# Attention on two row halves of the TensorE array: weighted sums on one half, float32 scores in 32-row strips on the other

## The chip, the cores and the metric

The kernel runs on one core of one Trainium2 chip. A core has a matrix engine (TensorE, "PE" in the profile, with its weight loads as "PEld"), a vector engine (VectorE, "DVE"), an activation engine (ScalarE, "ACT"), a general engine (GpSimd, "POOL") and SyncE ("SP"), which issues most of the DMAs here. Matrix products read SBUF and write PSUM, which has eight banks of 128 x 512 float32. The metric is the device time of one execution in microseconds (us); smaller is better. All inputs and outputs are float32.

## The reference

A block with two branches on the same normalised input, 2048 tokens of width 448: attention with 16 query heads of width 28 that share one key and one value head, and an MLP of width 1792 behind a second normalisation.

```python
def _A_ref(x, wq, wk, wv, wo):
    B, S, D = x.shape                       # 1, 2048, 448
    H = 16
    Dh = D // H                             # 28
    q = (x @ wq).reshape(B, S, H, Dh).transpose(0, 2, 1, 3)
    k = x @ wk
    v = x @ wv
    scores = jnp.einsum("bhqd,bkd->bhqk", q, k) * (Dh ** -0.5)
    p = _softmax(scores, axis=-1)
    o = jnp.einsum("bhqk,bkd->bhqd", p, v)
    return o.transpose(0, 2, 1, 3).reshape(B, S, H * Dh) @ wo

def _B_ref(x, w1, b1, w2, b2):
    y = _layernorm(x, axis=-1)
    h = _gelu(jnp.einsum("bsd,df->bsf", y, w1) + b1)
    return jnp.einsum("bsf,fd->bsd", h, w2) + b2

xn = _layernorm(x, axis=-1)
return x + _A_ref(xn, wq, wk, wv, wo) + _B_ref(xn, w1, b1, w2, b2)
```

## The kernel before

The program is written in one function, `block_kernel`, with the order of the instructions of each engine set by hand (`manual_schedule`). Matrix products that need float32 accuracy are done in two ways. Some take float32 operands as they are; the profile shows two records for each such product. Others split an operand into a high and a low half of the type float32r and add three products of halves, one record each.

**Projection** (0 to 66 us). For each of four chunks of 512 tokens, `norm_parts` normalises and transposes the rows, and `q_slot` computes four groups of 128 columns of queries, keys and values. Its `evac` copies a group's high half to `qe[:, 0, :]` (L396), and `low` subtracts to get the low half `qe[:, 1, :]` (L403). Group 0 holds the value and the key. Four DMAs spread the key's halves over four blocks of 32 rows of `ks` (high, high, low, low in an order that pairs with the queries' blocks), and the halves of the queries go to two tensors in DRAM, `qd[0]` and `qd[1]`.

**MLP** (66 to 352 us). 56 slots, each `mlp1` (eleven products into a bank of the ring `ra`, then the gelu on ScalarE and VectorE) and, two slots later, `mlp2` (twelve products into four banks that stay open). In the last two slots `then` puts a score behind each group of three products, eight scores in all (`EARLY`).

**Attention** (352 to 893 us). The work is cut into 16 units of four heads and 512 queries, a unit into 16 key tiles of 128 keys. For each key tile and head, `scores` does one product over all 128 rows (L616): the three products of halves, 28 rows each, and a row that carries the shift of the exponent stand one above the other in the 128 rows. It lands in a bank of the rings `ra` and `rb` (three each, taken in turn), and ScalarE turns it into weights with an exponential (L618), which are float32 in SBUF. `pv` multiplies the weights of a key tile by the values, 32 columns with a column of ones for the sum (L731): four float32 products, one for each head, each over 128 rows and on its own 32 columns of the array, all adding into the one bank `po`.

The loop (L820) goes in steps of two key tiles: eight scores, and then `weighted()` with the eight weighted sums of the step before. Small jobs hang on slots between the scores: the load of the next unit's queries (`load_unit`, eight DMAs), its running maximum over the first 32 keys (`find_max`, one product, L537, then VectorE and a DMA that writes the shift row), the normalisation of the last unit (`norm_jobs`: a copy out of the bank, a DMA of the sums, a reciprocal, two DMAs through DRAM that spread it, a multiplication and the split into halves), and the output projection (`o_parts`, twelve products of 448 columns a unit into the bank `mo`, L694 to L698, one to three a step as `PARTS` says). `last_norm` finishes the last unit. Behind it stands a branch (`outside`) that recomputes all units with the true maximum if a sum left its limits; in the execution profiled here it is not taken.

The scores' order, the wait for a bank and the weighted sums are these lines:

```python
s = score_bank()
pe.matmul(s, ks[:, kt * P:(kt + 1) * P], qss[u][:, j, :], start=True, stop=True)
p = early.pop(0) if early else att.tile([P, CW], F32, name="p", bufs=WEIGHTS)
act.activation(p, s, AF.Exp, scale=SCALE)
```

Of the kernel before, what the change touches and what calls it, by code (L numbers as in the profile page):

```python
# [18 lines left out]
P = 128  # L19
# [13 lines left out]
WEIGHTS = 28  # L33
EARLY = 8
PARTS = 2, 1, 2, 1, 2, 2, 2
# [4 lines left out]
def block_kernel(ctx, tc, x, wq, wk, wv, wo, w1, b1, w2, b2, out):  # L40
# [8 lines left out]
    mo = ctx.enter_context(tc.tile_pool(name="mo", bufs=1, space=PSUM))  # L49
# [63 lines left out]
    def bank(shape):  # L113
        return mo.tile(shape, F32, name="mo")

# [17 lines left out]
    make_identity(nc, ident)  # L133
    one = keep.tile([P, 3], F32, name="one")
# [5 lines left out]
    pool.memset(f(ks), 1.0)  # L140
    pool.memset(f(kd), 0.0)
    pool.memset(f(qm), 0.0)
# [129 lines left out]
    def norm_parts(c, second, first=False, bank=mtile):  # L272
        again, second = second, second or c in KEPT
        xh = xt_p.tile([P, 4, CW], F32R, name="xh")
        xl = xl_p.tile([P, 4, CW], F32R, name="xl")
        xts[c, second and c not in KEPT] = xh, xl
        xns = {}

        def center(k):
            t = CT * c + k  # L280
            if first:
                xn = f(wqp.tile([P, 2, CW], F32R, name="qe", bufs=5))[:, 0, :]
            else:
                xn = (wqp if k % 2 and not again else tmp).tile([P, 4 * P], F32, name="xn", bufs=1)
            scale, bias = (lnq, lnqb) if second else (lnr, lnb)
            src = lines.pop(t) if again else xin[t]
            act.activation(xn[:, 0:D], src, AF.Identity, bias=bias[:, t:t + 1], scale=scale[:, t:t + 1])
            xns[k] = xn

            def doubled():  # L290
                (pool if 0 < c else dve).tensor_scalar(
                    xn[:, D:512], src[:, 384:448], scale[:, t:t + 1], bias[:, t:t + 1], op0=ALU.mult, op1=ALU.add)

            if first and k == 1:
                return doubled
            doubled()

        def turn(k, lows=None):
            sl = slice(k * P, (k + 1) * P)
            pt = bank([P, 4, P])  # L300
            for b in range(4):
                pe.transpose(pt[:, b, :], xns[k][:, b * P:(b + 1) * P], ident)  # L302
            act.activation(xh[:, :, sl], pt, AF.Copy)
# [80 lines left out]
    def q_slot(c, i):  # L384
# [7 lines left out]
        def evac():  # L392
            qe = wqp.tile([P, 2, CW], F32R, name="qe", bufs=5)
            if c in KEPT:
                dve.tensor_mul(ps, ps, ibs[c])
            act.activation(qe[:, 0, :], ps, AF.Copy)  # L396
            vt = None
            if i == 0:
                vt = wqp.tile([32, CW], F32, name="vt", bufs=1)
                act.activation(vt, ps[0:32, :], AF.Copy)  # L400

            def low():
                dve.tensor_sub(qe[:, 1, :], ps, f(qe[:, 0, :]))  # L403
                if i == 0:
                    for dst, j in ((32, 0), (0, 1), (64, 1), (96, 0)):
                        nc.sync.dma_start(f(ks[dst:dst + DH, cols]), f(qe[32:60, j, :]))
                    for h in range(4 if c == 0 else 0):
                        nc.sync.dma_start(f(kd[32 * h:32 * h + DH, 32 * h:32 * h + 32]), f(qe[32:60, 0, 0:32]))
# [105 lines left out]
    qss, ots, qst = {}, {}, []  # L514

    def clear_q():
        qst.append(xt_p.tile([P, 4, CW], F32R, name="xh"))
        pool.memset(f(qst[-1]), 0.0)

    def load_q(u, qs):  # L520
        c, g = units[u]
        for blk, i in ((1, 0), (2, 0), (0, 1), (3, 1)):
            src = qd[i][4 * DH * g:4 * DH * (g + 1), c * CW:(c + 1) * CW].rearrange("(j r) n -> r j n", r=DH)
            nc.sync.dma_start(f(qs[32 * blk:32 * blk + DH]), src)

    def load_strips(u):
        c, g = units[u]
        for j in range(4):
            rs = slice(DH * (4 * g + j), DH * (4 * g + j + 1))
            nc.sync.dma_start(f(qm[32 * j:32 * j + DH, :]), qd[0][rs, c * CW:(c + 1) * CW])  # L530
# [4 lines left out]
    def block_max(keys, dst):  # L535
        pm = bank([P, CW])
        pe.matmul(pm, keys, qm, start=True, stop=True)  # L537
# [3 lines left out]
    def shift_rows(u, mr):  # L541
        mn = keep.tile([P, CW // 32], F32R, name="mn", bufs=2)
        dve.tensor_scalar(mn, mr, -1.0, 0.0, op0=ALU.mult, op1=ALU.add)
        dve.transpose(blocks(tm), f(mn)[:, :, None].to_broadcast([P, CW // 32, 32]))
        nc.sync.dma_start(f(qss[u][60:61, :, :]), tm[DH:P:32, :])

    def load_unit(u):
        qss[u] = qst[u % 2]
        load_strips(u)
        load_q(u, qss[u])  # L550

    def find_max(u):
        mr = keep.tile([P, CW // 32], F32, name="mr", bufs=2)
        block_max(kd, mr)
        shift_rows(u, mr)

    ring_a = ctx.enter_context(tc.tile_pool(name="ra", bufs=3, space=PSUM))
# [30 lines left out]
    def mlp2(c, ft, then=None):  # L588
# [5 lines left out]
        for k in range(CT):  # L594
# [8 lines left out]
            if then is not None:  # L603
                then()
# [4 lines left out]
    todo = [(u, kt, j) for u in range(NU) for kt in range(NT) for j in range(4)]  # L609

    def score_bank():
        return ring_b[0].tile([P, CW], F32, name="t") if ring_b and next(turn_s) % 2 else spare()

    def scores(u, kt, j):
        s = score_bank()
        pe.matmul(s, ks[:, kt * P:(kt + 1) * P], qss[u][:, j, :], start=True, stop=True)  # L616
# [10 lines left out]
    for n in range(len(mslots) + 2):  # L627
# [12 lines left out]
        if (c, ft) == (NCH - 1, 1):  # L640
            clear_q()
            clear_q()
# [10 lines left out]
        if n >= len(mslots):  # L653
            t = f(xl_p.tile([P, 4, CW], F32R, name="xl"))
            early.extend(t[:, k, :] for k in range(4))
            mlp2(*mslots[n - 2], then=lambda: scores(*todo.pop(0)))
# [6 lines left out]
    ring_b.append(ctx.enter_context(tc.tile_pool(name="rb", bufs=3, space=PSUM)))  # L663
    op = ctx.enter_context(tc.tile_pool(name="op", bufs=1, space=PSUM))
# [40 lines left out]
    def norm_jobs(u, po):  # L705
        c, g = units[u]
        oc = att.tile([P, CW], F32, name="oc")
        dve.tensor_copy(oc, po)  # L708
# [18 lines left out]
    def pv(u, kt):  # L727
        if kt == 0:
            pos[u] = op.tile([P, CW], F32, name="po")
        for j in range(4):  # L730
            pe.matmul(pos[u][32 * j:32 * j + 32, :], vs[:, kt, :], ps[u, kt, j],  # L731
                      start=(kt == 0), stop=(kt == NT - 1))
# [31 lines left out]
    side = {}  # L764

    def at(step, job, slot=4):
        side.setdefault((min(step, PER * NU - 1), slot), []).append(job)
# [9 lines left out]
    at(3, split_out)  # L777
    waiting = []

    def weighted():  # L780
        for u, kt in waiting:
            pv(u, kt)
        if not waiting or waiting[-1][1] < NT - 1 or u == NU - 1:
            return
        norm = norm_jobs(u, pos.pop(u))
        next(norm)
        for d in (1, 3):
            at(PER * (u + 1) + d, lambda: next(norm), 3)
        parts = []

        def part():
            if not parts:
                parts.append(o_parts(*units[u]))
            next(parts[0])

        for d, n in enumerate(PARTS if u < NU - 2 else (3, 3, 3, 3)):
            for slot in (1, 5, 7)[:n]:
                at(PER * (u + 1) + 4 + d, part, slot)
# [10 lines left out]
    def flag(last):  # L809
# [5 lines left out]
        pf = bank([1, 1])  # L815
# [3 lines left out]
    done = EARLY  # L819
    for step in range(PER * NU):  # L820
        for i in range(8):
            if done:
                done -= 1
            else:
                scores(*todo.pop(0))
            for job in side.pop((step, i), []):
                job()
        weighted()
        waiting = [divmod(n, NT) for n in (2 * step, 2 * step + 1)]
    extremes(sums[:, 0:NU - 1, :].rearrange("p u e -> p (u e)").bitcast(I32), worst)  # L830
    weighted()
    tc.mark_branch_hint_location("outside", hint="LikelyTaken")
    last_norm(NU - 1, pos.pop(NU - 1), flag)

    outside = nc.values_load(count)
    with tc.If(outside > 0, preferred_fallthrough_block=True, label="outside"):
        ka = att.tile([P, 8, P], F32R, name="ka", bufs=1)
        mx = att.tile([P, CW // 32, S // 32], F32, name="mx", bufs=1)
        pool.memset(f(ka), 0.0)
        for u in range(NU):  # L840
            load_unit(u)
            for n in range(S // 32):
                for h in range(4 if n % 8 == 0 else 0):
                    nc.sync.dma_start(f(ka[32 * h:32 * h + DH, :, 32 * h:32 * h + 32]),
                                      f(blocks(ks[32:32 + DH, 32 * n:32 * n + 256])))
                block_max(ka[:, n % 8, :], mx[:, :, n])
# [3 lines left out]
            for kt in range(NT):  # L850
                for j in range(4):
                    scores(u, kt, j)
                pv(u, kt)
            for _ in norm_jobs(u, pos.pop(u)):
# [28 lines left out]
```

## Time and profile before

| | us |
|---|---|
| median of 3 runs (lowest, highest) | 906.45 (904.81, 907.35) |
| the profiled execution | 906.6 |
| its span, from the first to the last instruction | 904.8 |
| projection | 0 to 66 |
| MLP | 66 to 352.4 |
| attention | 352.4 to 892.6 |
| end | 892.6 to 904.8 |

The columns of the lines below are told where they are shown. A record of a group names its line, engine, operation, what it writes and reads, its form, and its count; busy time and the mean of one instruction in ns follow. In the time-ordered view the first number is the start in us and the second the length; a bracket tells how long the engine was idle before and what ended that. The form of a matrix product is rows * columns of the array that it uses: 128*128 is the whole array, 128*32 one group of 32 columns. The ends of matrix products are modelled, so distances between starts are used for what one costs.

### The profile page before, as it was taken

How to read it: one execution, taken by the hardware profiler on the slowest of the kernel's cores; microseconds unless marked ns; L12 is line 12 of the kernel's file. 1: busy time of each engine (PE TensorE's matmuls, PEld its weight loads, DVE VectorE, ACT ScalarE, POOL GpSimd, SP SyncE). 2: the span in 40 equal slices, each digit the busy share in tenths (PEclk: the TensorE clock that was granted, in tenths of full speed). 3: DMA queues.
4: the chain of work that ended last, by engine and by line, in shares of the span. 5: the costliest groups of instructions: out<-in, count | busy, mean ns of one | idle time of the engine just before them, and what ended most of it. 6: DMA issues, size and time to landing. Idle time of an engine off the chain costs nothing.

```text
span 904.8 us, 13015 instructions
## 1 busy us (share of the span) xinstructions
PE 889.1 (98%) x4925; PEld 567.7 (63%) x4925; DVE 293.7 (32%) x554; ACT 676.6 (75%) x1285; POOL 156.4 (17%) x149
## 2 busy tenths in 40 slices
PE   8989999999999999999999999999999999999996
PEld 8867888888888887454454454455455455455452
DVE  7865455335345342222122122122122122122123
ACT  5764443433443437999999999999999999999993
POOL 6443343233235331000000000000000000000000
PEclk9999999999999999999999999999999999999999
DMA  9791112002001303402202222202222112232001
GB/s 299 203 280 49 42 62 82 1 0 82 19 23 52 71 11 106 112 26 54 50 26 54 76 82 54 50 25 54 81 76 54 48 29 54 73 84 54 1 13 45
DMA packets 42047, 60.08 MB, mean 66 GB/s; under 512 B 10795, under 2 KB 26745, under 8 KB 41977
## 3 DMA queue, kind: packets, MB, share of 16 engines
q1 hardware_dynamic: 40568, 58.60, 22.8%
q8 instruction: 41, 0.67, 0.3%
q10 hardware_dynamic: 1408, 0.57, 0.2%
q14 instruction: 30, 0.24, 0.1%
HBM read 43.16 MB, written 14.80 MB: 64 GB/s over the span
## 4 chain that ended last, share of the span: by engine, by line
PE 94%; DVE 2%; ACT 1%; issue 0%; DMA 0%; POOL 0%; ACTq 0%; DVEq 0%; POOLq 0%
PE po L731 26%; PE s L616 16%; PE m L596 14%; PE t L616 13%; PE s L178 12%; PE qp L178 3%; PE mo L694 1%; PE mo L696 1%; PE mo L698 1%; PE s L181 1%; PE s L183 1%; PE qp L302 0%; DVE hz L579 0%; PE mo L537 0%; PE qp L181 0%
## 5 line engine op out<-in xcount | busy, mean ns | idle before, releaser
L618 ACT ACTIVATE p<-s 128x512 f32<-128x512 f32 x508 | 315.5, 621 | 26.7 <-PE s L616 22.3
L618 ACT ACTIVATE p<-t 128x512 f32<-128x512 f32 x508 | 319.5, 629 | 0.0
L731 PE MATMUL po<-p,vs 128*32 128x512 f32 x2032 | 244.1, 598 | 0.0
L616 PE MATMUL s<-xh,ks 128*128 128x512 f32 x516 | 216.6, 420 | 0.0
L616 PE MATMUL t<-xh,ks 128*128 128x512 f32 x508 | 200.4, 394 | 0.3 <-DVE a L601 0.3
L616 PEld LDWEIGHTS s<-xh,ks 128*128 128x128 f32 x516 | 97.0, 188 | 121.6 <-ACT p L618 105.6
L731 PEld LDWEIGHTS po<-p,vs 128*32 128x32 f32 x2032 | 53.1, 109 | 121.4 <-issue 116.1
L577 ACT ACTIVATE hx<-s,b1t 128x512 f32<-128x512 f32 x56 | 38.5, 688 | 115.3 <-PE s L183 105.6
L700 DVE TENSOR_TENSOR row<-row,mo 128x448 f32<-128x448 f32 x60 | 37.3, 621 | 235.9 <-PE mo L698 234.7
L585 POOL TENSOR_TENSOR hl<-hx,hh 128x512 fp32r<-128x512 f32 x56 | 77.6, 1386 | 184.1 <-DVE hh L584 175.0
L722 POOL TENSOR_TENSOR otl<-oc,oth 128x512 fp32r<-128x512 f32 x15 | 19.4, 1292 | 500.5 <-DVE oth L721 266.3
L616 PEld LDWEIGHTS t<-xh,ks 128*128 128x128 f32 x508 | 95.5, 188 | 14.0 <-ACT p L618 1.9
L596 PE MATMUL m<-w2l,hh 128*128 128x448 f32 x224 | 82.6, 369 | 0.9 <-DVE w2l L380 0.9
L596 PE MATMUL m<-w2h,hl 128*128 128x448 f32 x224 | 82.0, 366 | 0.7 <-POOL hl L585 0.7
L596 PE MATMUL m<-w2h,hh 128*128 128x448 f32 x224 | 82.3, 367 | 0.2 <-DVE a L601 0.2
L579 DVE SCALAR_TENSOR_TENSOR hz<-hz,hx 128x512 f32<-128x512 f32 x56 | 45.3, 808 | 105.8 <-ACT hz L578 105.5
L580 ACT ACTIVATE hz<-hz 128x512 f32<-128x512 f32 x56 | 35.4, 632 | 49.4 <-DVE hz L579 49.4
L178 PE MATMUL s<-xh,w1h 128*128 128x512 f32 x168 | 66.1, 394 | 2.4 <-DVE qe L403 2.4
L178 PE MATMUL s<-xh,w1l 128*128 128x512 f32 x168 | 66.3, 395 | 0.0
L178 PE MATMUL s<-xl,w1h 128*128 128x512 f32 x168 | 66.3, 395 | 0.0
L581 DVE SCALAR_TENSOR_TENSOR hx<-hz,hx 128x512 f32<-128x512 f32 x56 | 39.1, 698 | 43.3 <-ACT hz L580 43.3
L708 DVE COPY oc<-po 128x512 f32<-128x512 f32 x15 | 10.4, 692 | 115.4 <-PE po L731 115.4
(162 smaller groups left out, 893.5 us busy)
## 6 DMA issues: line engine op xcount, KB each, us to landing
xh<-qd SPq DMA_DIRECT2D x64, 224.0 KB
qd<-qe SPq DMA_DIRECT2D x24, 256.0 KB
a<-in_A_x_dram SPq DMA_DIRECT2D x24, 224.0 KB
tr<-ld SPq DMA_DIRECT2D x60, 64.0 KB
ad<-a SPq DMA_DIRECT2D x16, 224.0 KB
qm<-qd SPq DMA_DIRECT2D x64, 56.0 KB
row<-ad SPq DMA_DIRECT2D x16, 224.0 KB
raw<-in_B_w_dram SPq DMA_DIRECT2D x7, 448.0 KB
```

The lines of the kernel that those rows point to most:

```text
L178: pe.matmul(ps, w, v, start=(n == 0), stop=False)
L577: act.activation(hx, ph, AF.Identity, bias=b1t[:, ft:ft + 1])
L579: dve.scalar_tensor_tensor(hz, hz, 1.0, hx, op0=ALU.add, op1=ALU.mult)
L580: act.activation(hz, hz, AF.Tanh, scale=GELU[1])
L581: dve.scalar_tensor_tensor(hx, hz, 1.0, hx, op0=ALU.add, op1=ALU.mult)
L585: pool.tensor_sub(hl, hx, f(hh))
L596: pe.matmul(m2[k], h[:, k * P:(k + 1) * P], w[:, ft, :], start=(ft == 0 and i == 0), stop=(ft == NF - 1 and i == 2))
L616: pe.matmul(s, ks[:, kt * P:(kt + 1) * P], qss[u][:, j, :], start=True, stop=True)
L618: act.activation(p, s, AF.Exp, scale=SCALE)
L700: dve.tensor_add(a, a, po)
L722: pool.tensor_sub(otl, oc, f(oth))
L731: pe.matmul(pos[u][32 * j:32 * j + 32, :], vs[:, kt, :], ps[u, kt, j], start=(kt == 0), stop=(kt == NT - 1))
```

## The change

The scores become plain float32 products over one strip of 32 rows: head j of a unit has its queries and its copy of the keys in the rows 32j to 32j+31. A weighted sum is cut into two halves of 64 keys, which add into two banks. The loop runs over blocks of four key tiles, each in two phases. In the first phase the scores of heads 2 and 3 of a block (rows 64 to 127) stand between the weighted sums over the keys 0 to 63 of the block before (rows 0 to 63); in the second the heads 0 and 1 and the keys 64 to 127.

With that, the low halves of keys and queries and the tensor `qd[1]` go, `find_max` becomes four products on 32-row strips, the bank `mo` goes and its users take banks from the scores' ring (four of `ra`, two of `rb`), the output products stand six in a row behind a phase, twice a unit, and the two accumulators are added (`norm_jobs`, `last_norm`). Sixteen scores instead of eight are done within the last two MLP slots, in four groups of four. A branch hint moves from the end to the start.

```diff
-WEIGHTS = 28
-EARLY = 8
-PARTS = 2, 1, 2, 1, 2, 2, 2
+WEIGHTS = 32
+B = 4
...
-    qd = [dram.tile([D, S], F32, name=f"qd{i}") for i in range(2)]
+    qd = dram.tile([D, S], F32, name="qd")
...
-    ks = keep.tile([P, S], F32R, name="ks")
-    kd = keep.tile([P, P], F32R, name="kd")
+    ks = keep.tile([P, S], F32, name="ks")
...
-    qm = keep.tile([P, CW], F32R, name="qm")
+    qst = [keep.tile([P, CW], F32, name=f"qs{i}") for i in range(2)]
...
+    tc.mark_branch_hint_location("outside", hint="LikelyTaken", engines=engines)
...
-            qe = wqp.tile([P, 2, CW], F32R, name="qe", bufs=5)
+            qe = wqp.tile([P, CW], F32, name="qe", bufs=5)
             if c in KEPT:
-                dve.tensor_mul(ps, ps, ibs[c])
-            act.activation(qe[:, 0, :], ps, AF.Copy)
-            vt = None
-            if i == 0:
-                vt = wqp.tile([32, CW], F32, name="vt", bufs=1)
-                act.activation(vt, ps[0:32, :], AF.Copy)
+                dve.tensor_mul(qe, ps, ibs[c])
+            else:
+                act.activation(qe, ps, AF.Copy)
+            vt = qe[0:32, :] if i == 0 else None
 
             def low():
-                dve.tensor_sub(qe[:, 1, :], ps, f(qe[:, 0, :]))
                 if i == 0:
-                    for dst, j in ((32, 0), (0, 1), (64, 1), (96, 0)):
-                        nc.sync.dma_start(f(ks[dst:dst + DH, cols]), f(qe[32:60, j, :]))
...
+                    for j in range(4):
+                        nc.sync.dma_start(ks[32 * j:32 * j + DH, cols], qe[32:60, :])
...
-                for j in range(2):
-                    nc.sync.dma_start(qd[j][rows, cols], f(qe[at, j, :]))
+                nc.sync.dma_start(qd[rows, cols], qe[at, :])
...
+    def strip(j, n=32):
+        return slice(32 * j, 32 * j + n)
+
+    def block_max(u, n, dst):
+        pm = score_bank()
+        for j in range(4):
+            pe.matmul(pm[strip(j), :], ks[strip(j, DH), 32 * n:32 * n + 32], qss[u][strip(j, DH), :], start=True, stop=True)
+        dve.transpose(tm, pm)
+        dve.tensor_reduce(dst, blocks(tm), axis=AX.X, op=ALU.max)
...
     def load_unit(u):
         qss[u] = qst[u % 2]
-        load_strips(u)
-        load_q(u, qss[u])
+        for j in range(4):
+            rs = slice(DH * (4 * g + j), DH * (4 * g + j + 1))
+            nc.sync.dma_start(qss[u][strip(j, DH), :], qd[rs, c * CW:(c + 1) * CW])
...
-    ring_a = ctx.enter_context(tc.tile_pool(name="ra", bufs=3, space=PSUM))
+    ring_a = ctx.enter_context(tc.tile_pool(name="ra", bufs=4, space=PSUM))
...
+    def block(n):
+        return [(n * B // NT, n * B % NT + i) for i in range(B)]
 
     def score_bank():
-        return ring_b[0].tile([P, CW], F32, name="t") if ring_b and next(turn_s) % 2 else spare()
+        return ring_b[0].tile([P, CW], F32, name="t") if ring_b and next(turn_s) % 3 == 2 else spare()
 
     def scores(u, kt, j):
         s = score_bank()
-        pe.matmul(s, ks[:, kt * P:(kt + 1) * P], qss[u][:, j, :], start=True, stop=True)
+        pe.matmul(s, ks[strip(j), kt * P:(kt + 1) * P], qss[u][strip(j), :], start=True, stop=True)
...
-            mlp2(*mslots[n - 2], then=lambda: scores(*todo.pop(0)))
+            mlp2(*mslots[n - 2], then=lambda k: k % 2 and [scores(0, 2 * (n - len(mslots)) + k // 2, j) for j in range(4)])
...
-    ring_b.append(ctx.enter_context(tc.tile_pool(name="rb", bufs=3, space=PSUM)))
-    op = ctx.enter_context(tc.tile_pool(name="op", bufs=1, space=PSUM))
+    ring_b.append(ctx.enter_context(tc.tile_pool(name="rb", bufs=2, space=PSUM)))
+    op = ctx.enter_context(tc.tile_pool(name="op", bufs=2, space=PSUM))
...
-            po = bank([P, D])
+            po = score_bank()[:, 0:D]
...
-        dve.tensor_copy(oc, po)
+        dve.tensor_copy(oc, pos.pop((u, 0)))
+        yield
+        dve.tensor_add(oc, oc, pos.pop((u, 1)))
...
-    def pv(u, kt):
+    def pv(u, kt, h):
         if kt == 0:
-            pos[u] = op.tile([P, CW], F32, name="po")
+            pos[u, h] = op.tile([P, CW], F32, name="po")
+        rows = slice(64 * h, 64 * h + 64)
         for j in range(4):
-            pe.matmul(pos[u][32 * j:32 * j + 32, :], vs[:, kt, :], ps[u, kt, j],
+            pe.matmul(pos[u, h][strip(j), :], vs[rows, kt, :], ps[u, kt, j][rows, :],
                       start=(kt == 0), stop=(kt == NT - 1))
 
-    def last_norm(u, po, flag):
+    def last_norm(u, flag):
         c, g = units[u]
+        po = att.tile([P, CW], F32, name="sum", bufs=1)
+        dve.tensor_copy(po, pos.pop((u, 0)))
+        dve.tensor_add(po, po, pos.pop((u, 1)))
...
-    PER = NT // 2
+    PER = 2 * NT // B
     for u in range(NU):
         c, g = units[u]
         if u + 1 < NU:
-            at(PER * u, lambda u=u: load_unit(u + 1))
-            at(PER * u + 3, lambda u=u: find_max(u + 1))
+            at(max(PER * u, 2), lambda u=u: load_unit(u + 1))
+            at(PER * u + 4, lambda u=u: find_max(u + 1))
...
+        norm, parts = norm_jobs(u), []
+        for d in (0, 1, 2, 3):
+            at(PER * (u + 1) + d, lambda norm=norm: next(norm))
+
+        def part(u=u, parts=parts):
             if not parts:
                 parts.append(o_parts(*units[u]))
-            next(parts[0])
+            for _ in range(6):
+                next(parts[0])
...
+        for d in (4, 5):
+            at(PER * (u + 1) + d, part)
...
-    done = EARLY
-    for step in range(PER * NU):
-        for i in range(8):
...
+    for n in range(1, NU * NT // B):
+        for h in range(2):
+            for now, past in zip(block(n), block(n - 1)):
+                for j in (2 - 2 * h, 3 - 2 * h):
+                    scores(*now, j)
+                pv(*past, h)
+            for job in jobs.pop(2 * n + h, []):
+                job()
     extremes(sums[:, 0:NU - 1, :].rearrange("p u e -> p (u e)").bitcast(I32), worst)
-    weighted()
-    tc.mark_branch_hint_location("outside", hint="LikelyTaken")
-    last_norm(NU - 1, pos.pop(NU - 1), flag)
+    for past in block(n):
+        for h in range(2):
+            pv(*past, h)
...
+    last_norm(NU - 1, flag)
```

More of the change, by code (lines that the diff above doesn't have):

```diff
@@ L133, in block_kernel @@
     make_identity(nc, ident)
+    engines = [getattr(mybir.EngineType, e) for e in ("PE", "Activation", "DVE", "Pool", "SP")]
+    tc.mark_branch_hint_location("outside", hint="LikelyTaken", engines=engines)
     one = keep.tile([P, 3], F32, name="one")
@@ L513, in block_kernel @@
     NU = len(units)
[L514 to L530, printed above, removed]
+    qss, ots = {}, {}
     def blocks(t):
         return t.rearrange("p (a b) -> p a b", b=32)
-    def block_max(keys, dst):
-        pm = bank([P, CW])
-        pe.matmul(pm, keys, qm, start=True, stop=True)
+    def strip(j, n=32):
[4 more added lines that the diff above has]
+            pe.matmul(pm[strip(j), :], ks[strip(j, DH), 32 * n:32 * n + 32], qss[u][strip(j, DH), :], start=True, stop=True)
         dve.transpose(tm, pm)
@@ L603, in mlp2 @@
             if then is not None:
-                then()
+                then(k)
     early = []
@@ L762, in last_norm, with at @@
             (nc.scalar if k % 2 else nc.sync).dma_start(ov[:, CT * c + k, :], a)
-    side = {}
-    def at(step, job, slot=4):
-        side.setdefault((min(step, PER * NU - 1), slot), []).append(job)
-    PER = NT // 2
+    jobs = {}
+    def at(phase, job):
+        jobs.setdefault(phase, []).append(job)
+    PER = 2 * NT // B
     for u in range(NU):
@@ L842, in block_kernel @@
             for n in range(S // 32):
[L843 to L846, printed above, removed]
+                block_max(u, n, mx[:, :, n])
             mr = keep.tile([P, CW // 32], F32, name="mr", bufs=2)
@@ L852, in block_kernel @@
                     scores(u, kt, j)
-                pv(u, kt)
-            for _ in norm_jobs(u, pos.pop(u)):
+                for h in range(2):
+                    pv(u, kt, h)
+            for _ in norm_jobs(u):
                 pass
```

64 lines of the change are left out of this document (18 added, 46 removed).

## The prediction

> **What bounds the kernel now.** I read the page's busy shares and its chain of work first, then the busy time by stretch, and then the time-ordered view of one step.
>
> ```profile
> PE 889.1 (98%) x4925; PEld 567.7 (63%) x4925; DVE 293.7 (32%) x554; ACT 676.6 (75%) x1285; POOL 156.4 (17%) x149
> ...
> PE 94%; DVE 2%; ACT 1%; issue 0%; DMA 0%; POOL 0%; ACTq 0%; DVEq 0%; POOLq 0%
> ```
> ```profile
> 0.00:66.00 66.00, 61.05 (x344) 50.80 (x344) 49.80 (x134) 44.03 (x77) 35.02 (x58) 1.00 0.85 258
> 66.00:352.40 286.40, 284.62 (x1312) 245.34 (x1313) 129.33 (x202) 120.66 (x190) 100.90 (x75) 0.99 0.14 42
> 352.40:892.60 540.20, 539.81 (x3261) 270.13 (x3260) 109.17 (x200) 511.32 (x1018) 19.37 (x15) 1.00 0.21 55
> 892.60:904.80 12.20, 3.66 (x10) 1.44 (x10) 5.41 (x18) 0.55 (x1) 1.13 (x1) 0.92 0.23 82
> ```
>
> TensorE is the chain (94%). The columns after the length are PE, PEld, DVE, ACT and POOL. The third stretch is attention: 540.2 us, 60% of the span. TensorE is busy throughout, but ScalarE, at 511 us, is close behind. How close is not in that sum, because its instructions overlap. Their starts tell it:
>
> ```profile
> 559.44 0.59 ACT L618 ACTIVATE p<-t 128x512 f32<-128x512 f32 x1
> ...
> 562.31 0.67 ACT L618 ACTIVATE p<-t 128x512 f32<-128x512 f32 x1
> 563.25 0.60 ACT L618 ACTIVATE p<-s 128x512 f32<-128x512 f32 x1 [0.28 <-PE s L616]
> ```
>
> Six intervals between the seven back-to-back exponentials of which the first two rows are the ends take 2.87 us, 0.478 each. The third row is the wait for a score, once a step. 1016 exponentials need at least 1016 x 0.478 = 486 us, so no gain on TensorE can take attention below that: 54 us is the most there is. Now one step on TensorE (eight scores, then the weighted sums of two key tiles):
>
> ```profile
> 560.54 0.39 PE L616 MATMUL t<-xh,ks 128*128 128x512 f32 x1
> 560.86 1.92 PE L731 MATMUL po<-p,vs 128*32 128x512 f32 x16
> 562.72 0.50 PE L616 MATMUL s<-xh,ks 128*128 128x512 f32 x1
> 563.05 0.39 PE L616 MATMUL t<-xh,ks 128*128 128x512 f32 x1
> 563.28 0.39 PE L616 MATMUL s<-xh,ks 128*128 128x512 f32 x1
> ```
> ```profile
> 561.32 0.13 PEld L731 LDWEIGHTS po<-p,vs 128*32 128x32 f32 x4 [0.30 <-issue]
> ...
> 561.75 0.13 PEld L731 LDWEIGHTS po<-p,vs 128*32 128x32 f32 x4 [0.30 <-issue]
> ```
>
> A score starts every 0.23 us. From the end of the last one (560.54 + 0.23 = 560.77) to where the next step's first would have started (563.05 - 0.23 = 562.82) are 2.05 us. The 16 records in them (two for each float32 product) go in four rounds of four, 0.43 us apart, together 1.72; the other 0.33 us are two changes of form, 0.165 each. A step is 8 x 0.23 + 2.05 = 3.89 us; 128 steps, with the 180 output products at 0.205 us and 15 maxima at 0.23, make 538 us, against 540.2 measured. ScalarE needs 8 x 0.478 = 3.83 for the same step.
>
> **The change, part by part.** *Attention.* A phase is half a block of four key tiles: eight scores in two strips, and 16 weighted sums of 64 keys. A score is now float32, so two records of 0.43 in its own strip; two strips side by side give 0.86 us a key tile. Four weighted sums use the four column groups, two rounds, 0.86. If the row halves work at once, a phase is 4 x 0.86 + 0.165 for changing places = 3.60 us on TensorE. ScalarE needs 3.83. So ScalarE sets it: 126 phases x 3.83 = 482.6 us.
>
> What no longer hides is the rest of TensorE's work. Output products went singly between scores; now six stand in a clump, twice a unit, in another form: 12 x 0.205 + 2 x 0.165 = 2.79 us. The running maximum is now float32: 0.86 + 0.165 = 1.03. A unit is then 8 x 3.60 + 3.82 = 32.6 us for TensorE alone, 30.6 for ScalarE alone, and 34.5 if ScalarE idles through all of it. Bounds: 2.0 to 3.8 above 30.6. The products now wait for banks of the scores' ring, and behind them in TensorE's order stand the next scores, for which ScalarE waits. Six banks hold at most about five waiting scores, 2.4 us of ScalarE; a refill takes 0.86 plus its latency of about 0.2. So the first clump and the maximum (2.4 us) expose about 1.2, and the second, which comes when TensorE has won back only 0.2 us, nearly all of its 1.4 and part of the refill. I take 3.0, x 15 = 45 us. First result and last sums: 3 us. Attention: 482.6 + 45 + 3 = 530.6, a gain of **9.6 us** (bounds: 25 gained to 2 lost).
>
> *Its other waits.* The normalisation runs through two DMAs:
>
> ```profile
> 557.07 0.25 DVE L713 RECIPROCAL rc<-rc 128x16 f32<-128x16 f32 x1
> 562.39 0.69 DVE L719 TENSOR_TENSOR oc<-oc,tr 128x512 f32<-128x512 f32 x1 [1.26 <-DMA tr<-ld]
> 563.71 1.29 POOL L722 TENSOR_TENSOR otl<-oc,oth 128x512 fp32r<-128x512 f32 x1 [29.79 <-PE s L616]
> ```
>
> From the reciprocal to the end of the low half are 7.9 us. It is issued one phase apart from the multiplication and two from the first clump: 2 x 3.83 = 7.7, and the product that needs the low half comes third, at 8.1. VectorE will wait about 1.5 us for the DMA, with nothing urgent queued behind; TensorE just does not. Zero, up to 0.5 x 15 = 7 if the DMA is later. SyncE issues four query loads a unit where it issued eight; they have a whole unit.
>
> *Before attention.* Sixteen scores instead of eight stand in the last two slots of the MLP:
>
> ```profile
> 346.54 0.39 PE L616 MATMUL s<-xh,ks 128*128 128x512 f32 x1
> 346.77 0.37 PE L596 MATMUL m<-w2h,hh 128*128 128x448 f32 x1
> 346.98 0.36 PE L596 MATMUL m<-w2l,hh 128*128 128x448 f32 x1
> ```
>
> Eight cost 8 x 0.23 = 1.8 us. Four groups of four strips cost 4 x (0.86 + 2 x 0.165) = 4.8. The four banks refill late: four exponentials end 3 x 0.478 + 0.62 us after the first starts, against six products at 0.205 between groups, so about 0.7 x 3 = 2 more. **+4.9** (2.9 to 6.5).
>
> *Projection.* The low halves of the queries go, with their subtraction, and half of the 256 KB stores. What that is worth is read where TensorE waits for it:
>
> ```profile
> 63.13 0.39 PE L183 MATMUL qp<-xl,wah 128*128 128x512 f32 x1
> 65.96 0.47 PE L178 MATMUL s<-xh,w1h 128*128 128x512 f32 x1 [2.44 <-DVE qe L403]
> ...
> 68.05 0.63 PE L178 MATMUL s<-xh,w1h 128*128 128x512 f32 x1
> 68.48 0.63 PE L178 MATMUL s<-xl,w1h 128*128 128x512 f32 x1
> ```
> ```profile
> 63.12 1.29 DVE L395 TENSOR_TENSOR qp<-qp,ib 128x512 f32<-128x512 f32 x2
> 64.52 1.29 DVE L403 TENSOR_TENSOR qe<-qp,qe 128x512 fp32r<-128x512 f32 x2
> ```
>
> Without L403 the banks come free at 64.41 instead of 65.81: 1.4 us. After the wait some eight products start 0.43 instead of 0.23 us apart, 1.7 us more; the 0 to 66 us stretch, with only shorter waits in it, shows a clock of 1.00, so I take that as gone. **-3** (0 to -3.2). Elsewhere the subtractions lie beside TensorE's work and cost nothing, as do the clears of GpSimd (two of 128x2048 go from the MLP, one of 128x512 comes at the start beside the first loads). The MLP gets a fourth bank; TensorE idles 1.8 us in that whole stretch, so it is worth 0 to 1.8, and I take 0.
>
> *End.* A copy and an addition of the two accumulators, each like
>
> ```profile
> L708 DVE COPY oc<-po 128x512 f32<-128x512 f32 x15 | 10.4, 692 | 115.4 <-PE po L731 115.4
> ```
>
> stand on the path after the last sum: **+1.4**. In the other units they have a phase each. The hint now stands at the start, beside the first loads: nothing, and if it is missed at the end, less than the 1.8 us around the span.
>
> Sum: -9.6 + 4.9 - 3 + 1.4 = -6.3. The profiled execution took 906.6 us (span 904.8 and 1.8 around it), the median is 906.45: **900 us**. With the bounds, this case runs from 884 to 917.
>
> **The rivals.** *One form at a time.* For it:
>
> ```profile
> 34.15 0.39 PE L183 MATMUL qp<-xl,wah 128*128 128x512 f32 x1
> 34.47 0.43 PE L419 MATMUL m<-ident,vt 32*128 32x32 f32 x4
> 34.83 0.66 PE L302 MATMUL qp<-ident,xn 128*128 128x128 f32 x4
> ```
> ```profile
> 34.46 0.32 PEld L419 LDWEIGHTS m<-ident,vt 32*128 32x128 f32 x4 [0.35 <-ACT xh L303]
> ```
>
> Within a form the next weights load while a product streams; at a change of form even the load waits, here until 0.31 us after the product's start, as at L731. Against it: both changes share rows, so they would have to wait anyway, and in the rounds of L731 column groups start together and none holds another up. If it holds for disjoint rows too, each of 504 half key tiles costs 0.86 + 0.165 + 0.86 + 0.165 = 2.05 us: 1033 + 57 + 3 = 1093 us of attention, **1463 us** in all. The change would then not do what it says. It decides from the first phase on. The Trainium skill (TensorEngine Tiling (Array Packing), Key Properties) has this rule: changing the tiling mode, not just the tile, drains the TensorE. By that rule the sum would be this one; the trace agrees where forms share rows, and shows no two forms on different rows.
>
> *Both at once, but stretched.* Three groups of rows write three banks where one was written, and six streams are read where four were. No row shows this. If a pass takes 0.50 instead of 0.43, a phase is 4.17 us, TensorE is the bound again with nothing covered: 126 x 4.17 + 57 + 3 = 585, **955 us**. Against it: weight loads, the obvious suspect, need at most 0.08 us for 128 columns (four of them within 0.32 in the row above). From a pass of about 0.45 on the gain is gone. The Trainium skill (TensorE: Matmul & The Clock Gate, Measured speedup vs the span model) gives 3.07 and not 4 for four row tiles; an estimate by it, passes 1.30 times as long, gives 126 x 4.64 + 60 = 645 and 1015 us. No run here shows that figure.
>
> *Better cover.* If the clumps hide down to TensorE's own 32.6 us a unit, attention is 15 us shorter: **885 us**.
>
> **How the numbers follow.** As forecast 0.54; one form at a time 0.17, for the only changes seen wait although all else overlaps, yet nothing shows disjoint rows; stretched 0.25; better cover 0.04. About 0.3% (2.7 us) is what a measurement can tell from no change. Of the forecast's 0.54, its bounds put 0.33 below 903.7, 0.11 within and 0.10 above 909.2; so faster 0.37, same 0.11, slower 0.52. The range leaves out the first rival and little else: 884 to 985. The likeliest case alone: 884 to 917.
>
> **What would show it.** Right: L616's strips and the weighted sums' records begin together, in rounds of 0.43; ScalarE's starts 0.478 apart in six phases of eight, with waits only behind the output products. Wrong: weighted sums that begin only where scores end; rounds longer than 0.45; a wait of TensorE for the low half of the normalised sums or for the shift row; the gap near 64 us still 2.4 us long.

## The result, and the profile after

| | us |
|---|---|
| before, median of 4 runs (lowest, highest) | 906.9 (904.8, 909.3) |
| after, median of 4 runs | 1464.35 (lowest 1463.99) |
| after / before | 1.6145, 95% interval 1.6114 to 1.6175 |
| predicted | 900, range 884 to 985 |
| the rival "one form at a time" | 1463 |

The changed kernel is 61% slower. Of its four runs one took 1543.8 us and had half the TensorE clock granted from 356 to 527 us; it is left out of the comparison, and the lines below are those of a further run of the changed kernel at full clock, 1462.27 us (span 1460.4).

The busy shares and the chain by engine and by line:

```profile
PE 1446.8 (99%) x8109; PEld 561.0 (38%) x8109; DVE 295.7 (20%) x555; ACT 707.9 (48%) x1269; POOL 152.6 (10%) x147
...
PE 97%; DVE 1%; ACT 1%; DMA 0%; issue 0%; POOL 0%; ACTq 0%; DVEq 0%; POOLq 0%
PE po L713 34%; PE s L598 24%; PE t L598 12%; PE m L576 9%; PE s L174 7%; PE qp L174 2%; PE s L515 1%; PE s L179 1%; PE s L177 1%; PE s L673 1%; PE t L673 1%; PE s L675 0%; PE s L677 0%; PE t L675 0%; PE t L677 0%; PE qp L298 0%
```

TensorE holds 97% of the chain, and 70% belongs to two lines: the weighted sums (L713) and the scores (L598, banks `s` and `t`). If they worked at the same time, their shares could not both stand in the chain in full. The busy time of the MLP and of attention (length, then PE, PEld, DVE, ACT, POOL) says which part grew:

```profile
63.30:351.20 287.90, 286.67 (x1336) 243.99 (x1336) 127.81 (x203) 121.92 (x194) 97.22 (x73) 1.00 0.12 38
351.20:1444.00 1092.80, 1092.80 (x6373) 263.64 (x6380) 119.47 (x216) 549.50 (x1014) 19.09 (x15) 1.00 0.05 15
```

The last weighted sums end at 1447.6 us, 3.6 us behind the second of these stretches, while the stretch of attention before held them: to the same point attention went from 540.2 to about 1096 us. The rest stands where it stood, a little shorter ahead of attention. ScalarE is busy for half of the stretch only. The time-ordered view of two half key tiles shows why, first TensorE's products, then ScalarE:

```profile
700.90 1.06 PE L713 MATMUL po<-p,vs 64*32 64x512 f32 x8
701.89 1.13 PE L598 MATMUL s<-qs,ks 32*128 32x512 f32 x4
702.95 1.06 PE L713 MATMUL po<-p,vs 64*32 64x512 f32 x8
```
```profile
699.44 0.59 ACT L600 ACTIVATE p<-s 128x512 f32<-128x512 f32 x1
701.00 0.60 ACT L600 ACTIVATE p<-s 128x512 f32<-128x512 f32 x1 [0.96 <-PE t L598]
701.49 0.59 ACT L600 ACTIVATE p<-t 128x512 f32<-128x512 f32 x1
703.05 1.09 ACT L600 ACTIVATE p<-s 128x512 f32<-128x512 f32 x2 [0.96 <-PE s L598]
```

Eight records of sums begin together, and the four of the scores begin only 0.99 us later, when the sums are through; the next sums come 1.06 us after that. No record of the one form starts among those of the other, though they use different rows; so it is from the first phase of the trace to the last, in 503 groups of each. A pair takes 2.05 us (700.90 to 702.95), and so it does on the mean of all. ScalarE gets two scores in a pair, works for 1.1 us and waits 0.96. What each weight load waits for agrees:

```profile
700.90 0.15 PEld L713 LDWEIGHTS po<-p,vs 64*32 64x32 f32 x8 [0.76 <-issue]
701.89 0.30 PEld L598 LDWEIGHTS s<-qs,ks 32*128 32x128 f32 x4 [0.84 <-ACT p L600]
```

Loads too begin only with the new form's products. The second row names an exponential as releaser. But with six banks and two scores to a pair a bank comes round every third pair, so the exponential that has to leave it had ended by 700.03 (699.44 + 0.59) at the latest, 1.9 us before the load: that is not what was waited for.

### The profile page after: what moved, and what is told of

The parts are those of the page before. It is cut to its first block, busy times and chain, and to the rows that moved or that the text cites. A ratio compares the mean times of both kernels' runs of the same rounds, so it can differ in the third digit from the quotient of the medians.

```text
span 1542.0 us, 19274 instructions
## 1 busy us (share of the span) xinstructions
PE 1528.2 (99%) x8109; PEld 572.1 (37%) x8109; DVE 295.7 (19%) x555; ACT 707.9 (46%) x1269; POOL 152.6 (10%) x147
## 4 chain that ended last, share of the span: by engine, by line
PE 98%; DVE 1%; ACT 1%; DMA 0%; issue 0%; POOL 0%; ACTq 0%; DVEq 0%; POOLq 0%
PE po L713 35%; PE s L598 25%; PE t L598 13%; PE m L576 9%; PE s L174 7%; PE qp L174 2%; PE s L515 1%; PE s L179 1%; PE s L177 1%; PE s L673 1%; PE t L673 1%; PE s L675 0%; PE s L677 0%; PE t L675 0%; PE t L677 0%; PE qp L298 0%
## 5 line engine op out<-in xcount | busy, mean ns | idle before, releaser
L598 PE MATMUL s<-qs,ks 32*128 32x512 f32 x1384 | 612.5, 680 | 0.0
L600 ACT ACTIVATE p<-s 128x512 f32<-128x512 f32 x676 | 384.1, 595 | 395.9 <-PE s L598 210.3
L713 PE MATMUL po<-p,vs 64*32 64x512 f32 x4032 | 561.6, 633 | 0.0
L598 PE MATMUL t<-qs,ks 32*128 32x512 f32 x664 | 398.9, 682 | 0.0
L600 ACT ACTIVATE p<-t 128x512 f32<-128x512 f32 x332 | 197.4, 595 | 227.1 <-PE s L598 227.1
L598 PEld LDWEIGHTS s<-qs,ks 32*128 32x128 f32 x1384 | 159.6, 192 | 296.0 <-ACT p L600 262.8
L713 PEld LDWEIGHTS po<-p,vs 64*32 64x32 f32 x4032 | 79.3, 107 | 405.3 <-issue 385.6
L598 PEld LDWEIGHTS t<-qs,ks 32*128 32x128 f32 x664 | 102.7, 193 | 154.9 <-ACT p L600 140.7
L679 DVE TENSOR_TENSOR row<-row,t 128x448 f32<-128x448 f32 x29 | 18.0, 622 | 264.4 <-PE t L677 264.4
```

What stands on the lines that cost most here:

```text
L598: pe.matmul(s, ks[strip(j), kt * P:(kt + 1) * P], qss[u][strip(j), :], start=True, stop=True)
L713: pe.matmul(pos[u, h][strip(j), :], vs[rows, kt, :], ps[u, kt, j][rows, :], start=(kt == 0), stop=(kt == NT - 1))
```

## The experiments

The theory was now that any change of form drains the array, whatever rows the two forms use. Its rivals: the two halves stand in each other's way because they stream and write banks at the same time, whatever their forms; or the order and the waits for banks make the alternation.

**One form only.**

```diff
-        rows = slice(64 * h, 64 * h + 64)
-        for j in range(4):
-            pe.matmul(pos[u, h][strip(j), :], vs[rows, kt, :], ps[u, kt, j][rows, :],
+        rows, k0 = strip(2 * h), kt - kt % 4
+        pe.matmul(pos[u, h], vs[rows, k0:k0 + 4, :].rearrange("p a b -> p (a b)"), ps[u, kt, 3][rows, :],
```

> The weighted sums of a half key tile become one product in the scores' own form, 32 rows by 128 columns, on a strip of the other half (it takes 32 of 64 keys and one of four heads, so most of the weighted sum is left out; its two records last as long as the four products did, two rounds of 0.43 us). The limits of the check on the sums are widened so that the branch is not taken. Theory 'one form at a time': with one form nothing drains, the product runs beside the scores, ScalarE sets a phase at 3.83 us, and the time is 1464 - (1033 - 483) = about 915, between 895 and 930. Rival 'the two row halves do not work at once': 0.86 + 0.86 = 1.72 us for a half key tile without the changes of form, 504 x 1.72 = 867, about 1298. Rival 'the weighted sums only wait in TensorE's order behind scores that wait for a bank': nothing changes but the form, about 1464.

It took 911.77 us, as the theory had it, beside 908.8 for the kernel before on the same chip. TensorE by time:

```profile
605.11 0.59 PE L598 MATMUL t<-qs,ks 32*128 32x512 f32 x1
605.12 0.59 PE L598 MATMUL s<-qs,ks 32*128 32x512 f32 x1
605.12 0.59 PE L712 MATMUL po<-p,vs 32*128 32x512 f32 x1
605.54 0.59 PE L598 MATMUL s<-qs,ks 32*128 32x512 f32 x1
605.55 0.59 PE L598 MATMUL t<-qs,ks 32*128 32x512 f32 x1
605.55 0.59 PE L712 MATMUL po<-p,vs 32*128 32x512 f32 x1
```

Two scores and a stand-in for the sums, on three strips of rows, begin within 0.01 us of each other, in rounds 0.43 us apart. Loop, waits, banks and jobs are those of the changed kernel: so neither order nor banks make the alternation. But the sums are also a quarter in number here, so this run alone does not show that the form is what did it.

**Forms that differ in columns alone, or in rows alone.** The first lets each sum read only one strip of 32 rows (`rows = strip(2 * h)`, with the sums 32*32 and the scores 32*128). The second splits a score into four products of 32 keys, so that scores are 32*32 and sums 64*32:

```diff
-        pe.matmul(s, ks[strip(j), kt * P:(kt + 1) * P], qss[u][strip(j), :], start=True, stop=True)
+        for i in range(4):
+            pe.matmul(s[strip(i), :], ks[strip(j), kt * P + 32 * i:kt * P + 32 * i + 32], qss[u][strip(j), :], start=True, stop=True)
```

> The weighted sums keep 32 columns but use 32 rows, one strip of the other half (32 of 64 keys; half of the weighted sum is left out), so that their form differs from the scores' in the columns alone: 32 by 32 against 32 by 128. If any difference of form empties the array: 2.05 us for each half key tile as in the changed kernel, 1464 (1450 to 1475). If only the rows of a form matter: they overlap, about 915. Rival 'row halves never overlap': 1464 as well, told apart by the first run.

> Each score is cut into four products of 32 keys, in the form 32 by 32; the weighted sums stay 64 by 32. The forms differ in the rows alone, and all of the result is computed. If any difference of form empties the array: 2.05 us for each half key tile, 1464 (1450 to 1480; four times as many score records, but four run side by side as the weighted sums do). If only the columns of a form matter: they overlap, ScalarE sets the phase, about 915 (up to 960 if the many records cost issue time).

The times were 2353.22 and 1441.06 us. TensorE of the first by time, then its clock over the span in 40 slices:

```profile
602.63 1.93 PE L713 MATMUL po<-p,vs 32*32 32x512 f32 x8
604.49 2.08 PE L598 MATMUL s<-qs,ks 32*128 32x512 f32 x4
```
```profile
PEclk9999995555555555555555555555555555555555
```

The two forms alternate as before: 604.49 - 602.63 = 1.86 us and then the other. The forecast of the time missed by far, because half the clock was granted through nearly all of attention (0.52 on the mean of 360 to 2340 us); I had not foreseen that. TensorE of the second:

```profile
601.98 1.06 PE L714 MATMUL po<-p,vs 64*32 64x512 f32 x8
602.97 1.09 PE L599 MATMUL s<-qs,ks 32*32 32x512 f32 x16
603.99 1.06 PE L714 MATMUL po<-p,vs 64*32 64x512 f32 x8
```

Alternation again, 2.01 us a pair, which is also why the time lies a little under the forecast's 1450 to 1480. A difference in columns alone is enough, and so is one in rows alone.

**The order alone.** Four strips of scores, then both halves of the sums; the operations are those of the changed kernel, and each form has the array to itself for a whole key tile. The small jobs hang behind the second or the fourth key tile of a block, in place of behind a phase (the diff leaves these lines out).

```diff
-        for h in range(2):
-            for now, past in zip(block(n), block(n - 1)):
-                for j in (2 - 2 * h, 3 - 2 * h):
-                    scores(*now, j)
+        for i, (now, past) in enumerate(zip(block(n), block(n - 1))):
+            for j in range(4):
+                scores(*now, j)
+            for h in range(2):
                 pv(*past, h)
...
```

> The order alone is changed: for each key tile first the scores of all four strips, then the weighted sums of both row halves, so that no two forms are meant to overlap, and a key tile changes form twice and not four times. Theory 'one form at a time': 0.86 + 0.165 + 0.86 + 0.165 = 2.05 us for a whole key tile, 252 x 2.05 = 517 in place of 1033, plus up to 15 us where both accumulators must be emptied between units: 948 to 965. Rival 'row halves do not work at once': strips or sums of the two halves run one after the other, 2 x 1.72 + 0.33 = 3.77 us a key tile, about 1380.

It took 988.21 us, some 23 more than the upper end. By time:

```profile
601.30 0.69 PE L598 MATMUL t<-qs,ks 32*128 32x512 f32 x1
...
602.38 1.09 PE L713 MATMUL po<-p,vs 64*32 64x512 f32 x16
603.39 0.70 PE L598 MATMUL s<-qs,ks 32*128 32x512 f32 x2
...
604.13 0.59 PE L598 MATMUL s<-qs,ks 32*128 32x512 f32 x1
604.65 1.09 PE L713 MATMUL po<-p,vs 64*32 64x512 f32 x16
```

Now sixteen records of sums, both row halves, take the 1.01 us that eight took before: one form does work on disjoint rows at once, with the very sums of the change. With the first run, where products for scores and sums shared the array in one form, that settles the theory: the same operations in another order save 474 us of 1462. A key tile takes 2.27 us here and 2.21 on the mean, not 2.05; over 252 key tiles the difference is the 40 us that the run lies above the lower end of its forecast. The scores are what is longer: their records start one by one until 604.13 instead of in two rounds. The likely reason is that each needs a bank that an exponential has to leave first.

**Two key tiles to a turn.** To see whether banks do that, the next run has the same order with eight scores, then two key tiles of sums: half the changes of form, and eight banks wanted where six are.

> The order of e4_strips_then_sums with two key tiles to a turn: eight scores, then the sums of both halves over two key tiles; nothing left out. If changes of form are all that e4_strips_then_sums loses, a turn is 4 x 0.86 + 0.33 = 3.77 us, under ScalarE's 3.83: 910 to 935 us. If the banks decide (six, for eight scores at once), the last two scores wait for two exponentials, and end about 3.2 us after the first began; with 1.72 + 0.33 us of sums a turn is about 5, so 252 x 0.25 = 60 us more than e4_strips_then_sums: about 1050.

It took 1093.39 us, 105 more than with one key tile to a turn though it changes form half as often. TensorE:

```profile
608.02 1.97 PE L713 MATMUL po<-p,vs 64*32 64x512 f32 x32
609.93 0.69 PE L598 MATMUL t<-qs,ks 32*128 32x512 f32 x1
...
612.76 0.59 PE L598 MATMUL s<-qs,ks 32*128 32x512 f32 x1
613.27 1.97 PE L713 MATMUL po<-p,vs 64*32 64x512 f32 x32
```

With one change of form each, 0.165 us, the sums take 1.91 us, as reckoned (1.72 + 0.165), and the eight scores 3.34 instead of the same 1.89; a turn is 5.25 us. Banks decide, as the second theory had it, with a price higher than its 60 us.

**All of it in one form.** Scores as in the second diff, each sum split into strips of 32 keys, so that everything is 32*32. It needs four accumulators, which leave four banks for scores.

```diff
-        rows = slice(64 * h, 64 * h + 64)
-        for j in range(4):
-            pe.matmul(pos[u, h][strip(j), :], vs[rows, kt, :], ps[u, kt, j][rows, :],
-                      start=(kt == 0), stop=(kt == NT - 1))
+        for r in (2 * h, 2 * h + 1):
...
+            for j in range(4):
+                pe.matmul(pos[u, r][strip(j), :], vs[strip(r), kt, :], ps[u, kt, j][strip(r), :],
+                          start=(kt == 0), stop=(kt == NT - 1))
```

> The whole of the change's work in one form: each score as four products of 32 keys, each weighted sum of 64 keys as two of 32 keys, so that scores and weighted sums are both 32 by 32, into four accumulators (one for each strip), which leaves four banks for the scores' ring where the change had six. All of the result is computed. Theory 'one form at a time': scores and weighted sums overlap; TensorE needs 0.86 us for a half key tile, ScalarE sets the phase at 3.83 us or a little more with four banks (up to 4.1), and the clumps of output products hide nothing: 126 x 3.83 to 4.1 + 57 to 65 us of attention, 905 to 950 in all. Rival 'work of different kinds does not overlap' or 'the many records cost issue time': 126 x 2 x 3.44 = 867, about 1295 or more.

> As the run with everything 32 by 32, but the twelve output products of a unit stand three behind each of four phases, not six behind each of two. Two more pairs of changes of form a unit cost 2 x 0.33 x 15 = 10 us of TensorE; against that a clump of 0.95 us fits the time that the ring covers. If exposure of the clumps is what is left above ScalarE's bound: 10 to 25 us faster than the run with two clumps. If four banks cover nothing: up to 10 us slower.

Both missed: 986.02 us, and 999.38 with the output products spread in threes. The changes of form that the four short clumps add were reckoned at 10 us, which is most of these 13. Scores and sums do overlap:

```profile
610.59 0.74 PE L599 MATMUL s<-qs,ks 32*32 32x512 f32 x8
610.76 0.73 PE L715 MATMUL po<-p,vs 32*32 32x512 f32 x8
611.01 0.74 PE L599 MATMUL s<-qs,ks 32*32 32x512 f32 x8
611.21 0.70 PE L715 MATMUL po<-p,vs 32*32 32x512 f32 x8
```

With 32*32 scores beside 64*32 sums the two alternated and took 1441 us; with the sums cut into the same form they overlap, and all of the result is still computed. What kept the time from 905 to 950 was to be told by the first experiment with the same four banks:

> The kernel of e1_one_form (one 32*128 product in place of the weighted sums; most of the weighted sum left out, limits widened) with a ring of four banks for the scores instead of six, as e5_all_32x32 has. If the ring is what made e5_all_32x32 86 us longer than forecast for it at best, this run is as long: 960 to 1000 us, with ScalarE's starts further apart than 0.478 us on the mean of a phase. If the 32*32 products with twice the streams are what made it so, this run stays at 911 to 925.

It took 959.12 us, just under the lower edge of what banks alone would make. The busy time of 400 to 850 us, all within attention, compares them; the count behind ACT is that of its exponentials. In order: the kernel before, one form with six banks, one form with four, and all in 32*32 with four:

```profile
400.00:850.00 450.00, 450.00 (x2720) 226.55 (x2712) 91.52 (x170) 426.44 (x849) 16.78 (x13) 1.00 0.20 54
```
```profile
400.00:850.00 450.00, 449.86 (x2779) 252.83 (x2774) 100.96 (x186) 413.67 (x840) 16.52 (x13) 1.00 0.09 28
```
```profile
400.00:850.00 450.00, 450.00 (x2556) 241.07 (x2558) 92.80 (x170) 387.59 (x771) 15.22 (x12) 1.00 0.09 27
```
```profile
400.00:850.00 450.00, 449.48 (x12049) 274.16 (x12024) 105.38 (x186) 383.52 (x738) 15.37 (x12) 1.00 0.10 29
```

An exponential takes 0.530 us of the stretch before (450 / 849), then 0.536, 0.584 and 0.610. Four banks instead of six cost 0.048 x 1016 = 49 us, against 47 measured between those two runs (959.1 and 911.8). That is more than half of the 74 between 911.8 and 986.0. The other 27 come with the full number of products in 32*32; whether they are streams that slow each other, more weight loads, or scores that now stand behind sums, no run tells apart. No version here beats the kernel before. Scores of 128 rows as it has them, but in 128*32 like its sums, would do without changes of form as well, and weren't tried: as plain float32 products a score would take two rounds of 0.43 us instead of its 0.23 (an estimate from the rounds of L731), and the halves of float32r were not run in that form.

## Why the prediction was wrong

**The step that failed** is "If the row halves work at once, a phase is 4 x 0.86 + 0.165 = 3.60 us on TensorE." Its condition does not hold for this pair: row halves do work at once in one form, but in none of the three pairs of forms that were run did two forms work at once, although their rows were disjoint. Everything that followed from it (ScalarE sets the phase, the clumps, 530.6 us of attention) describes a kernel that this is not. The sign named beforehand, "weighted sums that begin only where scores end", is what the trace shows from the first phase to the last.

**What stood in its place** is the rival, term by term: 0.86 + 0.165 + 0.86 + 0.165 = 2.05 us for half a key tile, 2.05 measured; 57 us for output products and maxima, 57.4 measured; 1093 us of attention, about 1094 measured from the end of the early scores (some 353.5) to that of the last sums (1447.6); 1463 in all, 1464 measured. The price of a change was in the trace of before (0.33 us in a step, two changes), and so was the row of L419 whose weight load waited at a change of form. By the drain rule of the Trainium skill (TensorEngine Tiling (Array Packing), Key Properties) the sum was this one, and the runs agree with it: 988 us against 1462 for the same operations, by order alone.

**The weighing** was wrong, then, not the working. I held against the rival that column groups start together in the rounds of L731. But those are one form: they say that tiles of a form overlap, and nothing on two forms. The changes of form in the trace's attention, two a step through 540 us, cost 0.165 us each on the mean; none is seen to be free. On that evidence the rival deserved more than the forecast had.

**"Both at once but stretched"** did not come about. Nor is a stretch seen where four strips are at work: in the order experiment the first key tile's scores began at 601.30 and its sums at 602.38, 1.08 us for two rounds and a change, where 0.43 a round makes 1.03 and passes 1.30 times as long would make 1.28.

**ScalarE's bound and the clumps** can be read from the one-form run, which has them without the alternation. Its waits for TensorE between 400 and 850 us (us in total, times, longest):

```profile
ACT p L600 <- PE po L712: 38.1, 27, 2.1
```

In 450 us, which are 840 / 64 = 13.1 units, ScalarE waited 38.1 us: 2.9 a unit, where I took 3.0. Between the waits an exponential took (450 - 38.1) / 840 = 0.490 us, not 0.478: 0.012 x 1016 = 12 us that I had not counted. The prediction misread its own rows here: it took the distance of starts. From the end of the first exponential (559.44 + 0.59) to that of the seventh (562.31 + 0.67) are 2.95 us, 0.49 each; the lengths grow from 0.59 to 0.67, as the starts run ahead of the ends. ScalarE's least is then 1016 x 0.490 = 498 us, and at most 42 us were there to gain, not 54. So even where the row halves do work at once, with a quarter of the sums, the time is 911.8 and not 900: these 12 us alone are more than the 6.3 that the forecast had to gain.

**The terms beside attention.** In the last MLP slots the groups of early scores:

```profile
342.98 1.14 PE L598 MATMUL s<-qs,ks 32*128 32x512 f32 x8
344.05 0.47 PE L576 MATMUL m<-w2h,hh 128*128 128x448 f32 x1
...
345.47 1.91 PE L598 MATMUL s<-qs,ks 32*128 32x512 f32 x8
347.30 0.48 PE L576 MATMUL m<-w2h,hh 128*128 128x448 f32 x1
...
351.22 3.42 PE L598 MATMUL s<-qs,ks 32*128 32x512 f32 x12
354.57 1.06 PE L713 MATMUL po<-xl,vs 64*32 64x512 f32 x8
```

The first group costs 1.07 us, the second 1.83, with 0.76 of waiting for banks, as forecast (0.7); the third (348.73 to 349.80) is again 1.07 long. The fourth stands behind the last product of the MLP, in one row with the first two scores of the loop: 3.35 us, of which those two take 1.06, so some 2.3. From the first of these slots to the end of the last early score are then about 11.8 us (341.67 to some 353.5), against 6.72 before (345.93 to 352.65): **+5.1** where I had 4.9. Without the subtraction the MLP begins earlier:

```profile
63.37 0.50 PE L174 MATMUL s<-xh,w1h 128*128 128x512 f32 x1 [0.78 <-DVE qe L391]
63.71 0.39 PE L174 MATMUL s<-xl,w1h 128*128 128x512 f32 x1
63.94 0.40 PE L174 MATMUL s<-xh,w1l 128*128 128x512 f32 x1
```

That is 2.6 us sooner (65.96 before): the wait is 0.78 us instead of 2.44, and the projection's last product starts at 62.20 instead of 63.13, 0.9 us that I had put at nothing. The products behind the wait are 0.23 apart from the second on, not 0.43; the clock granted from 63 to 71 us was 0.79 before and is full now. From here to the first of the last slots are 278.3 us instead of 280.0. In all about **-4.3** stands against -3: the step was right, and its bound of -3.2 too narrow.

At the end the copy and the addition of the two accumulators are there, 0.69 us each. First the kernel before, then the changed one:

```profile
888.82 3.64 PE L731 MATMUL po<-p,vs 128*32 128x512 f32 x32
892.60 0.45 DVE L745 STREAM_TRANSPOSE tr<-po 128x256 f32<-128x256 f32 x1 [2.43 <-PE po L731]
```
```profile
1443.07 4.50 PE L713 MATMUL po<-p,vs 64*32 64x512 f32 x72
1446.84 0.69 DVE L719 COPY sum<-po 128x512 f32<-128x512 f32 x1 [17.83 <-PE po L713]
1447.63 0.69 DVE L720 TENSOR_TENSOR sum<-sum,po 128x512 f32<-128x512 f32 x1
1448.35 0.45 DVE L730 STREAM_TRANSPOSE tr<-sum 128x256 f32<-128x256 f32 x1
```

The copy runs beside the last sums of the other accumulator, so only the addition stands on the path: from the end of the last sums to the first transposition are 0.78 us instead of 0.14, **+0.6** and not 1.4. Together these terms make 1.4 us where the forecast had 3.3; it is partly luck that the rival's total came within 2 us. (The forecast's own lower bounds add up to 883 us, not 884.)

## What to carry to other kernels

Concurrency of tiles has to be shown for the pair of forms that is planned: tiles of one form on different rows or columns run together, but each change of form cost 0.165 us on the mean and emptied the array here, so group work by form, and count changes before anything else. Fewer changes want more scores waiting in banks, and where banks run out first that costs more than the changes saved (1093 against 988 us). When every instance of a thing in the trace pays a price, take it as the likeliest that the next one pays too, however good the reason why it should not.

## What the runs showed of the hardware

- A form is both numbers, rows and columns. 64*32 beside 32*32 alternated (2.01 us a pair), and so did 32*32 beside 32*128 (1.86 and 2.01 us in turn, at half the clock), all on disjoint rows.
- In the run with 32*32 sums on one strip the granted clock was 0.52 on the mean of 360 to 2340 us, though TensorE is counted as busy for 1977 of these 1980 us. The full clock came back 17 times, for 3 to 7 us each, and each time 2.9 to 4.9 us after the start of one of the 30 clumps of six output products, which use the whole array. In the execution of 1543.8 us of the changed kernel the full clock came back, at 526.9, 3.8 us after the start of the first such clump (523.1). The share of the array in use might thus be what counts; but 13 of the 30 clumps brought nothing, and no run varied that share alone.
- Records of different tiles within one form need not start in the order of the program: in the one-form run the records of a float32 product start 0.43 us apart, with those of other strips between them.
